# RWKV attention and capacity-limited experts: the attention output kept in fp32 columns, cast per expert, with grams in halves and logits in spare PSUM columns

## The chip, the cores and the metric

One core of one Trainium2 chip. The time is the device time of one execution in microseconds (us); each run gives its own time, and a profile of one execution is a little shorter than the time of that run. Below, "time" is the median over runs, and "span" is the length of the profiled execution.

## The reference, cut to what matters

```python
def _attn_ref(r, k, v, w, u):            # r, k, v, w: (4, 8, 768, 48), u: (8, 48)
    for t in range(S):
        cur = einsum('bhd,bhe->bhde', u[None] * kt, vt)
        y[:, :, t] = einsum('bhd,bhde->bhe', rt, state + cur)
        state = wt[:, :, :, None] * state + einsum('bhd,bhe->bhde', kt, vt)

def _moe_ref(x, w_gate, w1, w2):         # x: (3072, 384), E = 8, F = 1024, cap = 384
    logits = x @ w_gate
    # greedy over all (token, expert) pairs by falling logit: a token goes to the
    # first expert that still has room; each expert takes exactly 384 tokens
    ...
    for e in range(E):
        h = np.maximum(x[mask] @ w1[e], 0.0)
        out[mask] = h @ w2[e]
```

So there are three stages: an attention scan that yields x, an assignment that needs all logits, and eight experts that each gather 384 rows of x, apply two products, and scatter the rows.

## The kernel before

The engines are named as the profile names them: PE is TensorE, ACT is ScalarE, DVE is VectorE, POOL is GpSimd. Tiles whose names end in `ps` lie in PSUM, where the products of PE are written; the others lie in SBUF. The attention works in 24 units (6 chunks of 128 positions, 4 batches each). In a unit, the gram is the product of its transposed keys and receptances, the mask copy takes the allowed part of it out of PSUM, and the intra products apply that part to the values. Every engine has its own list of operations, ordered by a key: unit number times a period, plus an offset for the kind of operation. The parts that the change touches, with cuts marked:

```python
# attention, per unit u
add("G", u, "PE", ...)        # gram: 32 matmuls into Gps
add("MS", u, "DVE", ...)      # mask copy of the whole gram, Gps -> M
add("Y", u, "PE", ...)        # intra products from M, then the last state product, into Yps
add("XE", u, "ACT", ..., fn=lambda u=u: nc.scalar.copy(             # contiguous, fp32
        out=XF[slot(("xf", u))][:112].rearrange("p s j t -> p s (j t)"),
        in_=Yps[:112, :, :256]))
add("XB", u, "ACT", ..., fn=lambda u=u: nc.scalar.copy(             # cast to bf16 columns
        out=xTb[:112, u].rearrange("p (s t) j -> p s j t", s=2),
        in_=XF[slot(("xf", u))][:112]))
...                                          # logits from XF, in a transpose tile (Tps)

# zeroes in the weight tiles of the later experts, then their loads (issued on GpSimd)
for e in range(NEARLY, E):                   # NEARLY = 3
    weights[e] = weight_tiles(wp, e)
    nc.scalar.activation(out=weights[e][0][32:64], ..., func=AF.Copy, scale=0.0)
    for fn in _weight_loads(nc, e, *weights[e], moe_w1, moe_w2):
        fn()

# experts
def gather(e):
    xe = xes[e] = xp.tile([128, NPAIR, CAP], BF16, name="xe", tag="xe")
    for k in range(2):
        nc.gpsimd.indirect_copy(
            xe[:, :, k * 192:(k + 1) * 192].rearrange("p j s -> p s j"), data, ...)
def up(e): ...      # 8 groups of 4 matmuls, 4 PSUM tiles hps; relu on ScalarE and VectorE in turn
def down(e): ...    # 3 groups of 8 matmuls, copy to osb, scatter (indirect DMA issued on GpSimd)

gather(0)
gather(1)
for e in range(E):
    up(e)
    if e + 2 < E:
        gather(e + 2)
    if e:
        down(e - 1)
down(E - 1)
```

## Time and profile before

The median was 437.4 us.

| stage (profile of before, span 441.3 us) | from | to |
|---|---|---|
| attention, up to the start of the last copy of logits | 0 | 159.4 |
| assignment, up to the ready index tile | 159.7 | 203.6 |
| experts, from the ready index on | 203.6 | 441.3 |

The page's summary rows. In section 2 each digit is the busy share of one of 40 equal slices (11 us each) in tenths; PEclk is the granted clock of TensorE in tenths.

```profile
span 441.3 us, 9730 instructions
...
PE   3878289898997663442060829370823708239000
...
POOL 8987835555559624420344433424335243352220
PEclk9999769999999655555566778685685956759655
```

Two things are to be seen: a weak slice near 50 us in which PE drops to 2 and the clock to 7 and 6 after it, and an expert stage in which PE comes in bursts while POOL is never quite idle.

Groups by line (line, engine, operation, output<-input, shapes, count, then busy us and mean ns of one, then the engine's idle time just before it and who ended it):

```profile
L725 PE MATMUL hps<-xe,w 112*128 112x384 bf16 x256 | 63.2, 426 | 111.5 <-POOL xe L715 111.5
L715 POOL INDIRECT_COPY xe<-xTb,idx 128x768 bf16 x16 | 61.8, 3864 | 106.2 <-issue 106.2
L428 ACT CAST xTb<-xf 112x512 bf16<-112x512 f32 x24 | 32.4, 1352 | 1.1
L424 ACT COPY xf<-yps 112x512 f32<-112x512 f32 x24 | 14.1, 587 | 27.8 <-PE yps L384 27.6
```

PE waits 111.5 us for gathered rows: POOL sets the pace of the expert stage. The gather is shown with 3.86 us, and nearly as much again stands as "issue" in front of it. "Perfetto Trace Analysis" of the Trainium skill (section "GPSIMD Engine Instruction") says to time such instructions by their start-to-start spacing. The trace agrees that this is needed: gathers in a row start 9.72 us apart while some 3.9 us is shown. The timeline of POOL around one expert (start, duration, then in brackets the idle time before and what ended it):

```profile
269.28 3.90 POOL L715 INDIRECT_COPY xe<-xTb,idx 128x768 bf16 x1 [5.82 <-issue]
279.00 3.91 POOL L715 INDIRECT_COPY xe<-xTb,idx 128x768 bf16 x1 [5.82 <-issue]
282.77 1.09 POOL L745 DMA_INDIRECT out_dram<-osb,tok_i  x1
286.25 1.00 POOL L745 DMA_INDIRECT out_dram<-osb,tok_i  x1 [2.39 <-issue]
289.63 0.97 POOL L745 DMA_INDIRECT out_dram<-osb,tok_i  x1 [2.38 <-PE hps L725]
296.90 3.85 POOL L715 INDIRECT_COPY xe<-xTb,idx 128x768 bf16 x1 [6.30 <-issue]
```

The first scatter follows the gather with no wait. In the attention, the waits view between 40 and 65 us names the cause of the weak slice (who waits, for whom, us in total, times, the longest):

```profile
PE tps L437 <- DMA wgT<-in_moe_w_gate_dram: 9.3, 2, 5.9
```

The pace of the attention is read from the copies out of yps. Those of unit 7 and of unit 19, twelve units apart:

```profile
67.60 0.59 ACT L424 COPY xf<-yps 112x512 f32<-112x512 f32 x1 [0.48 <-PE yps L384]
...
131.44 0.59 ACT L424 COPY xf<-yps 112x512 f32<-112x512 f32 x1
```

(131.44 - 67.60) / 12 = 5.32 us per unit (by chunks of four units it varies from 5.0 to 5.5). Last, VectorE between the two stages: the assignment (nl) starts straight after the last logits.

```profile
159.43 0.19 DVE L451 COPY logits_sb<-tps 128x32 f32<-128x32 f32 x1 [4.97 <-PE tps L448]
159.71 0.26 DVE L495 TENSOR_SCALAR nl<-logits_sb 128x192 f32<-128x192 f32 x1
```

### The profile page before, as it was taken

Reading aid. Unit: us, or ns where it says so; the run is one execution under the profiler, and the core shown is the slowest. Engines: PE = TensorE matmul, PEld = TensorE weight load, DVE = VectorE, ACT = ScalarE, POOL = GpSimd, SP = SyncE. Lnnn points to the kernel's source line nnn. Section 1 sums busy time; section 2 is a strip of 40 time slices with the busy share of each in tenths; the row PEclk is TensorE's granted clock in tenths of the full one; section 3 lists DMA queues with packets and bytes.
Section 4 is the critical chain, followed back from the end, with each engine's and each line's share of the span. In section 5 each row is a group of like instructions: output and inputs, shape, how many; then the busy total and the mean of one; then the engine's idle time right before and its main releaser. Section 6 shows DMA issues by size and latency. Waiting matters only on the chain. (4 is left out here: it accounts for less than half of the span.)

```text
span 441.3 us, 9730 instructions
## 1 busy us (share of the span) xinstructions
PE 238.5 (54%) x4221; PEld 151.9 (34%) x4221; DVE 149.0 (34%) x379; ACT 141.5 (32%) x196; POOL 206.8 (47%) x177
## 2 busy tenths in 40 slices
PE   3878289898997663442060829370823708239000
PEld 2556166566665531231030415140411404115000
DVE  4666238776785437664010202020200202003000
ACT  3687348776886379000010102010100102001000
POOL 8987835555559624420344433424335243352220
PEclk9999769999999655555566778685685956759655
DMA  9997999898408989998000000000100001001110
GB/s 167 171 175 141 178 184 172 157 186 159 77 3 129 202 121 186 192 202 120 0 0 0 0 0 2 18 36 0 56 0 18 36 0 54 1 18 72 56 53 19
DMA packets 113918, 37.06 MB, mean 84 GB/s; under 512 B 101328, under 2 KB 109648, under 8 KB 113872
## 3 DMA queue, kind: packets, MB, share of 16 engines
q1 hardware_dynamic: 100432, 19.09, 24.3%
q0 software_dynamic: 13440, 17.31, 21.6%
q8 instruction: 35, 0.57, 0.5%
q14 instruction: 11, 0.09, 0.1%
HBM read 44.25 MB, written 4.72 MB: 111 GB/s over the span
## 5 line engine op out<-in xcount | busy, mean ns | idle before, releaser
L725 PE MATMUL hps<-xe,w 112*128 112x384 bf16 x256 | 63.2, 426 | 111.5 <-POOL xe L715 111.5
L715 POOL INDIRECT_COPY xe<-xTb,idx 128x768 bf16 x16 | 61.8, 3864 | 106.2 <-issue 106.2
L725 PEld LDWEIGHTS <-w 112*128 112x128 bf16 x256 | 31.5, 123 | 144.0 <-issue 136.1
L728 DVE TENSOR_SCALAR hsb<-hps 128x384 bf16<-128x384 f32 x32 | 17.9, 558 | 159.6 <-PE hps L725 159.6
L730 ACT ACTIVATE hsb<-hps 128x384 bf16<-128x384 f32 x32 | 15.7, 491 | 165.6 <-PE hps L725 165.6
L314 POOL TENSOR_TENSOR mm<-diag,dd 128x512 f32<-128x512 f32 x24 | 25.7, 1071 | 42.1 <-DVE dd L309 20.4
L745 POOL DMA_INDIRECT out_dram<-osb,tok_i x24 | 23.6, 985 | 46.0 <-DMA out_dram<-osb,tok_i 21.4
L326 PE MATMUL tps<-ident,krs 128*112 128x128 f32 x192 | 33.3, 298 | 4.2 <-DVE krs L295 3.0
L331 ACT COPY krT<-tps 112x512 f32<-112x512 f32 x48 | 30.2, 629 | 8.6 <-PE tps L326 8.4
L428 ACT CAST xTb<-xf 112x512 bf16<-112x512 f32 x24 | 32.4, 1352 | 1.1
L738 PE MATMUL ops<-w,hsb 128*128 128x384 bf16 x192 | 32.4, 326 | 0.0
L690 POOL DMA_DIRECT2D w<-in_moe_w_dram x32 | 18.6, 583 | 25.9 <-DMA w<-in_moe_w_dram 13.7
L301 POOL TENSOR_TENSOR rku<-kr 128x384 f32<-128x384 f32 x24 | 24.1, 1004 | 1.4 <-DMA kr<-in_r_dram 1.2
L403 DVE COPY_PREDICATED mm<-mask,gps 128x512 f32<-128x512 uint8 x24 | 17.4, 726 | 21.0 <-PE gps L398 14.7
L305 POOL TENSOR_TENSOR rku<-rku,u_bc 128x384 f32<-128x384 f32 x24 | 24.1, 1004 | 0.3
L326 PEld LDWEIGHTS tps<-ident,krs 128*112 128x112 f32 x192 | 20.9, 140 | 8.8 <-POOL rku L301 3.7
L384 PE MATMUL yps<-krT,sm 48*48 48x64 f32 x384 | 22.5, 233 | 2.2 <-issue 1.5
L282 PE MATMUL cps<-ww,negut 128*128 128x384 f32 x48 | 21.4, 529 | 4.3 <-ACT ww L242 4.3
L295 DVE TENSOR_TENSOR krs<-kr,cps 128x768 f32<-128x768 f32 x24 | 22.7, 946 | 2.3 <-ACT cps L290 2.0
L384 PE MATMUL yps<-krT,st 48*48 48x64 f32 x384 | 22.4, 233 | 1.9 <-issue 1.9
L738 PEld LDWEIGHTS <-hsb 128*128 128x128 bf16 x192 | 18.8, 98 | 12.4
L424 ACT COPY xf<-yps 112x512 f32<-112x512 f32 x24 | 14.1, 587 | 27.8 <-PE yps L384 27.6
(144 smaller groups left out, 389.7 us busy)
## 6 DMA issues: line engine op xcount, KB each, us to landing
w<-in_moe_w_dram POOLq DMA_DIRECT2D x32, 192.0 KB, 10.1
w<-in_moe_w_dram POOLq DMA_DIRECT2D x8, 768.0 KB, 13.0
ww<-in_w_dram SPq DMA_DIRECT2D x24, 192.0 KB, 4.9
kr<-in_k_dram SPq DMA_DIRECT2D x24, 192.0 KB, 4.6
kr<-in_r_dram SPq DMA_DIRECT2D x24, 192.0 KB, 4.7
vv<-in_v_dram SPq DMA_DIRECT2D x24, 192.0 KB, 5.0
out_dram<-osb,tok_i POOLq DMA_INDIRECT x24, 2.6
u_bc<-in_u_dram SPq DMA_DIRECT2D x1, 192.0 KB, 4.3
```

Source lines behind the costliest of these rows:

```text
L295: fn=lambda u=u, kr=kr, b=b: nc.vector.tensor_tensor(out=KR[slot(("kr", u))][:, :, :, :D], in0=kr[:, :, b, :].rearrange("t x (h d) -> t x ...
L301: fn=lambda u=u, kr=kr, b=b: nc.gpsimd.tensor_tensor(out=P[slot(("p", u))], in0=kr[:, 0, b, :], in1=kr[:, 1, b, :], op=ALU.mult))
L305: fn=lambda u=u: nc.gpsimd.tensor_tensor(out=P[slot(("p", u))], in0=P[slot(("p", u))], in1=u_bc, op=ALU.mult))
L314: fn=lambda u=u: nc.gpsimd.tensor_tensor(out=M[slot(("m", u))], in0=_free(diag, [0, 2], [0, NPAIR], [1, 64]), in1=_free(Dg[slot(("dg", u)) ...
L326: nc.tensor.transpose(t[:112, at:at + 128], pair_of(s[:, x], j), ident)
L331: nc.scalar.copy(out=KRT[slot(("krt", u))][:112, 2 * half:2 * half + 2].rearrange("p j x t -> p (j x t)"), in_=Tps[slot(("t", u, half))][: ...
L384: mm(Yps[q * 64:q * 64 + D, half, j * 64:(j + 1) * 64], lhsT=s, rhs=t[cc * 64:cc * 64 + D, j, 1, half * 64:half * 64 + 64], start=(i == 0 ...
L428: fn=lambda u=u: nc.scalar.copy(out=xTb[:112, u].rearrange("p (s t) j -> p s j t", s=2), in_=XF[slot(("xf", u))][:112]))
L715: nc.gpsimd.indirect_copy(xe[:, :, k * 192:(k + 1) * 192].rearrange("p j s -> p s j"), data, idx16[:, e * 24 + k * 12:e * 24 + (k + 1) * 1 ...
L725: nc.tensor.matmul(hps, lhsT=w1sb[:112, jj, f8 * 128:(f8 + 1) * 128], rhs=xe[:112, jj, :], start=(jj == 0), stop=(jj == 3))
L738: nc.tensor.matmul(ops_, lhsT=hsb[:, f8, pc * 128:(pc + 1) * 128], rhs=w2sb[:, f8, :], start=(f8 == 0), stop=(f8 == FC - 1))
L745: nc.gpsimd.indirect_dma_start(out=out, out_offset=bass.IndirectOffsetOnAxis(ap=tok_i32[:, j:j + 1], axis=0), in_=osb, in_offset=None)
```

## The change

Its intent: drop the second pass over the attention output (the bf16 cast), let the gather move whole fp32 columns of four neighbouring values, and cast only what an expert needs; let PE start the intra products after half a gram; free the transpose tiles of logits. The keys of the schedule were tuned again with it. The diff, cut to its core:

```diff
-        add("MS", u, "DVE", 730, after=[op["G", u], op["DG", u]], ...)     # one gram, mask copy, intra
+        for i in range(2):                                                 # two halves of each
+            add(f"G{i}", u, "PE", 290, gram, ...)
+            add(f"MS{i}", u, "DVE", 430, after=[op[f"G{i}", u], op["DG", u]], ...)
...
-        add("XE", u, "ACT", 590, ... XF ..., in_=Yps[:112, :, :256]))
-        add("XB", u, "ACT", 620, ... xTb ...)
+        add("XE", u, "ACT", 620, after=[op["Y1", u]], give=[("y", u)],
+            fn=lambda u=u: nc.scalar.copy(
+                out=xT[:, u].rearrange("p (s t) j -> p s j t", s=2),       # fp32, 16-byte stride
+                in_=Yps[:, :, :256].rearrange("p s (j t) -> p s j t", j=NPAIR)))
...
-                t = Tps[slot(("l", c))]                       # logits in a transpose tile
+                t = Ctail[0]                                  # spare columns of the cumsum tile
...
-            add("SW", u, "DVE", 500, ...)                     # state times decay
+            add("SW", u, "POOL", 600, ...)
...
     def gather(e):
         xe = xes[e] = xp.tile([128, NPAIR, CAP], BF16, name="xe", tag="xe")
         for k in range(2):
-            nc.gpsimd.indirect_copy(xe[...].rearrange("p j s -> p s j"), data, ...)
+            at = slice(k * 192, (k + 1) * 192)
+            x4 = gp.tile([128, 192, NPAIR], FP32, name="x4", tag="x4")
+            nc.gpsimd.indirect_copy(x4, data, ...)
+            flip = x4.rearrange("p s j -> p j s")
+            nc.vector.tensor_copy(out=xe[:, :2, at], in_=flip[:, :2])
+            nc.scalar.copy(out=xe[:, 2:, at], in_=flip[:, 2:])
...
     gather(0)
-    gather(1)
     for e in range(E):
+        if e + 1 < E:
+            gather(e + 1)
         up(e)
-        if e + 2 < E:
-            gather(e + 2)
         if e:
             down(e - 1)
...
-NEARLY = 3
+WT_AT = [30.0 + 0.01 * i for i in range(10)]                  # weights of the first two experts
+NEARLY = 2
...
-            nc.scalar.activation(out=weights[e][0][32:64], ..., func=AF.Copy, scale=0.0)
+            nc.vector.memset(weights[e][0][32:64], 0.0)
```

## The prediction

> **What bounds the kernel now.** Three stages, read from the timeline.
>
> Attention, 0 to 160 us. The q/k/v/w loads run at a DMA share of 0.9 to 1.1 until 113 us; from 62 us on PE is 18 of 20 us busy and one unit (the copy out of yps) takes 5.3 us. A hole at 45 to 62 us: the first logits matmul waits 9.3 us for the gate weights, queued behind loads (waits view).
>
> Assignment, 160 to 204 us: a DVE chain of short instructions.
>
> Experts, 205 to 433 us: POOL alone. PE waits 111.5 us for xe. Gathers end 9.72 us apart (shown as 3.85 busy after 5.86 "issue"), three scatters cost 8.2 us; 16 gathers (155 us) and 24 scatters follow each other without a gap. ACT and DVE are mostly idle there.
>
> **What the change does, by stage.**
>
> Attention. It removes the cast to xTb (24 x 1.35 us ACT), the xTb memsets (10.7 us POOL), 128-column transposes for four-column results, and the gate-weight hole. Halved grams let PE start the intra products earlier. SW moves to POOL, which has room. The logits leave the tps buffers. Against it: the yps copy now writes fp32 at a stride of 16 bytes, and the logits matmul reads at that stride. The cast, which writes bf16 at a stride of 8 bytes, takes 1.35 us where the same-sized plain copy takes 0.59; I estimate 0.6 to 1.1 us for the strided fp32 copy. Loads alone need 113 us, PE about 4.7 us per unit. Estimate: logits complete at 140 us (133 to 150) instead of 160.
>
> Between stages. Six zero memsets of expert weights move from ACT to DVE, ahead of the assignment in DVE's order. The built order shows 2048 elements each. "VectorE: DVE Perf Modes" of the Trainium skill (section on zero memsets) says one cycle per element: an estimate of 2.2 us each, 13 us on the critical path. Before they cost nothing (ACT, 17.6 us, idle engine). So about 7 us of the attention gain remain.
>
> Experts. Two opposite terms.
> (a) The gather writes contiguous fp32 instead of bf16 at a stride of 768 bytes. I read 5.86 us as fetching and 3.85 us as writing, 5 ns for each of 768 elements, slow like the strided bf16 cast on ACT. Contiguous writes should cut it: estimate 6.9 us per gather, saving 45 us over 16.
> (b) The casts of expert e+1 stand before the relus of expert e on DVE and ACT. Only four hps buffers exist, so up(e) stops after four groups until gather e+1 has landed; then cast 0.6, relu 0.5, four groups of 1.0, the first down group 1.4 and its copy 0.6 pass before the first scatter of e-1. Estimate: POOL now waits 7 us per expert, six times, 43 us. Before, the scatters followed at once.
> So the expert stage comes out about even; it is 40 us longer if the gather does not get faster.
>
> **Prediction:** 431 us, range 411 to 476. Faster by over 2%: 0.45; within 2%: 0.27; slower: 0.28.
>
> **What would show it.** Right: gather spacing near 7 us; POOL idle about 7 us before the first scatter of each expert; DVE 13 us in memsets before the assignment; no hole at the first logits; units nearer 5 us; last logits near 140 us. Wrong: gather spacing still 9.7 us (about 475 us); the yps copy at 1.4 us or more, with PE waiting for it; logits matmuls far above 1.9 us per chunk; POOL not waiting at the scatters.
>
> **What would make it wrong.** The gather's write phase may be a software loop indifferent to stride and type. The strided fp32 copy may cost more than the cast it replaces and hold yps, so that attention gains nothing. The granted clock, 0.5 to 0.76 outside steady attention, scales (b).

## The result, and the profile after

The kernel after takes 470.64 us (468.41 to 473.04, 4 runs) against 437.67 us. The ratio is 1.0745, 95% interval 1.0659 to 1.0832: slower. Ratios here and below are the mean time of one kernel's runs over that of the other's of the same rounds, so not quite the ratio of the medians quoted. Executions over 1.5% slower than the fastest of the same kernel are left out of the means.

```profile
span 471.3 us, 9781 instructions
...
PE   4786888888888603344046450620902705308900
...
POOL 4689283835657264310101020111120210210320
PEclk9997999969999855555565795675765956856965
```

POOL's digits in the expert stage fell from mostly 2 to 4 down to 0 to 3, and yet the stage is longer. The groups that answer to those of before:

```profile
L733 PE MATMUL hps<-xe,w 112*128 112x384 bf16 x256 | 62.1, 415 | 136.5 <-ACT hsb L738 119.0
L724 DVE CAST xe<-x 128x384 bf16<-128x384 f32 x16 | 39.8, 2486 | 109.5 <-POOL x L720 109.5
L720 POOL INDIRECT_COPY x<-xT,idx 128x768 f32 x16 | 17.2, 1077 | 119.8 <-issue 113.4
L432 ACT COPY xT<-yps 128x512 f32<-128x512 f32 x24 | 26.3, 1098 | 37.4 <-PE yps L386 37.4
```

The gather itself shrank to 1.08 us shown. PE no longer waits for the gather but for a relu of its own expert on ScalarE (119.0 us). The timeline of POOL around one expert says why:

```profile
319.13 1.08 POOL L720 INDIRECT_COPY x<-xT,idx 128x768 f32 x1 [6.30 <-issue]
327.34 1.07 POOL L720 INDIRECT_COPY x<-xT,idx 128x768 f32 x1 [7.13 <-issue]
337.86 1.01 POOL L753 DMA_INDIRECT out_dram<-osb,tok_i  x1 [9.45 <-DVE osb L752]
341.29 0.97 POOL L753 DMA_INDIRECT out_dram<-osb,tok_i  x1 [2.42 <-issue]
344.64 0.97 POOL L753 DMA_INDIRECT out_dram<-osb,tok_i  x1 [2.38 <-DMA out_dram<-osb,tok_i]
351.91 1.07 POOL L720 INDIRECT_COPY x<-xT,idx 128x768 f32 x1 [6.31 <-issue]
```

POOL stands still for 9.45 us before the first scatter. The casts of expert e+1 stand ahead of the relus of expert e in the order of ScalarE and VectorE, so up(e) stops once its four PSUM tiles are full, until gather e+1 has landed. Only then do relu, the second half of up(e), down(e-1) and the scatter follow, and meanwhile POOL has nothing to do. Six such waits: 8.68, 7.82, 9.45, 8.31, 8.02 and 9.27 us, 51.6 us in all. VectorE between the stages:

```profile
162.26 0.19 DVE L453 COPY logits_sb<-cps 128x32 f32<-128x32 f32 x1 [0.67 <-PE cps L450]
162.93 1.76 DVE L926 MEMSET w<- 32x2048 uint32 x1 [0.48 <-DVE logits_sb L453]
...
173.64 1.76 DVE L926 MEMSET w<- 32x2048 uint32 x1 [0.38 <-issue]
175.43 0.26 DVE L496 TENSOR_SCALAR nl<-logits_sb 128x192 f32<-128x192 f32 x1
```

Where the 30.0 us between the two spans lie, each from the starts and ends in the two traces and rounded by itself:

| piece | before | after | change, us |
|---|---|---|---|
| up to the start of the last logits copy | 159.4 | 162.3 | +2.8 |
| from there to the start of the assignment | 0.3 | 13.2 | +12.9 |
| assignment | 43.9 | 43.5 | -0.4 |
| index ready to the end of the first gather | 11.2 | 8.4 | -2.8 |
| end of the first gather to the end of the last | 177.9 | 196.7 | +18.7 |
| end of the last gather to the end | 48.5 | 47.2 | -1.3 |

In the attention, the hole at the first logits is gone, but PE waits for the mask copies twice in a unit. The waits view of PE in 60 to 150 us:

```profile
PE gps L347 <- DVE mm L409: 9.0, 16, 0.6
PE yps L423 <- DVE mm L409: 4.8, 14, 0.4
```

In the same view of before these two waits were 2.8 us (8 times, L345) and 2.1 us (twice, L416): 4.9 us, now 13.8 us. There is also a new hole near 37 us: a zero memset of weights (3.50 us) stands in POOL's order ahead of an operand that the mask copy needs. First POOL's line, then PE's:

```profile
34.51 3.50 POOL L906 MEMSET w<- 32x4096 bf16 x1
...
40.63 1.11 PE L423 MATMUL yps<-mm,vv 64*48 64x64 f32 x32 [3.81 <-DVE mm L409]
```

In this profile the clock was at half speed for two stretches of the attention, about 39 to 46 us and 97 to 107 us.

### The profile page after: what moved, and what is told of

Same layout as the page of the kernel before. It is cut to its first block, busy times and chain, and to the rows that moved or that the text cites. A ratio compares the mean times of both kernels' runs of the same rounds, so it can differ in the third digit from the quotient of the medians.

```text
span 471.3 us, 9781 instructions
## 1 busy us (share of the span) xinstructions
PE 240.8 (51%) x4247; PEld 156.2 (33%) x4247; DVE 190.8 (40%) x407; ACT 117.7 (25%) x183; POOL 158.0 (34%) x190
## 5 line engine op out<-in xcount | busy, mean ns | idle before, releaser
L733 PE MATMUL hps<-xe,w 112*128 112x384 bf16 x256 | 62.1, 415 | 136.5 <-ACT hsb L738 119.0
L724 DVE CAST xe<-x 128x384 bf16<-128x384 f32 x16 | 39.8, 2486 | 109.5 <-POOL x L720 109.5
L720 POOL INDIRECT_COPY x<-xT,idx 128x768 f32 x16 | 17.2, 1077 | 119.8 <-issue 113.4
L725 ACT CAST xe<-x 128x384 bf16<-128x384 f32 x16 | 13.9, 867 | 149.7 <-POOL x L720 149.7
L432 ACT COPY xT<-yps 128x512 f32<-128x512 f32 x24 | 26.3, 1098 | 37.4 <-PE yps L386 37.4
L409 DVE COPY_PREDICATED mm<-mask,gps 128x256 f32<-128x256 uint8 x48 | 20.8, 443 | 33.2 <-PE gps L402 17.6
L333 ACT COPY krT<-tps 112x512 f32<-112x512 f32 x48 | 28.7, 600 | 17.6 <-PE tps L328 16.6
L328 PEld LDWEIGHTS tps<-ident,krs 128*112 128x112 f32 x192 | 23.8, 147 | 12.7 <-issue 7.4
L423 PE MATMUL yps<-mm,vv 64*48 64x64 f32 x768 | 21.1, 229 | 12.9 <-DVE mm L409 11.6
L284 PE MATMUL cps<-ww,negut 128*128 128x384 f32 x48 | 22.9, 563 | 7.7 <-ACT ww L245 6.8
L746 PEld LDWEIGHTS <-hsb 128*128 128x128 bf16 x192 | 19.3, 101 | 13.8 <-issue 2.1
L292 ACT ACTIVATE cps<-cps 128x768 f32<-128x768 f32 x24 | 19.2, 802 | 16.6 <-PE gps L402 9.1
## 6 DMA issues: line engine op xcount, KB each, us to landing
w<-in_moe_w_dram POOLq DMA_DIRECT2D x8, 768.0 KB, 13.8
```

The source lines that it names most:

```text
L284: mm(Cps[:, 0, :DX], lhsT=negut, rhs=ww[:, b, :], start=True, stop=True)
L328: nc.tensor.transpose(t[:112, at:at + 128], pair_of(s[:, x], j), ident)
L333: nc.scalar.copy(out=KRT[slot(("krt", u))][:112, 2 * half:2 * half + 2].rearrange("p j x t -> p (j x t)"), in_=Tps[slot(("t", u, half))][: ...
L432: fn=lambda u=u: nc.scalar.copy(out=xT[:, u].rearrange("p (s t) j -> p s j t", s=2), in_=Yps[:, :, :256].rearrange("p s (j t) -> p s j t", ...
L724: nc.vector.tensor_copy(out=xe[:, :2, at], in_=flip[:, :2])
L733: nc.tensor.matmul(hps, lhsT=w1sb[:112, jj, f8 * 128:(f8 + 1) * 128], rhs=xe[:112, jj, :], start=(jj == 0), stop=(jj == 3))
```

## The experiments

Theory 1: the loss in the expert stage is the order of the casts. Theory 2: 13 us of it are the memsets on VectorE. Theory 3, on the attention: some part of the rework costs as much as the rest gains. The rivals are named in each expectation. The first four ran beside before at 438.67 us (437.96 to 439.36, 7 runs).

### e_late_casts: the casts of expert e+1 after the work of e

```diff
-            flip = x4.rearrange("p s j -> p j s")             # in gather(): cast at once
+            x4s[e].append(x4)
+    def cast(e): ...                                          # the same two casts per half
     gather(0)
+    cast(0)
     for e in range(E):
         ...
         up(e)
         if e:
             down(e - 1)
+        if e + 1 < E:
+            cast(e + 1)
```

> The changed kernel with one edit: the two casts of expert e+1 stand after the relus and copies of up(e) and down(e-1) in DVE's and ACT's order, no longer before them. Theory 1 (the casts' place in the order holds up POOL): the 7.8 to 9.5 us that POOL waits before the first scatter of experts 0 to 5 (51.6 us in all) vanishes, so about 420 us, 50 us less than the changed kernel. Rival (PE's up and down work itself is what the scatters wait for, whatever the order): the wait stays above 4 us per expert and the time stays above 445 us.

Measured: correct, 426.79 us (423.71 to 429.04, 4 runs), ratio 0.9706 (0.9666 to 0.9745). The scatter follows the gather at once:

```profile
264.69 1.08 POOL L719 INDIRECT_COPY x<-xT,idx 128x768 f32 x1 [6.51 <-issue]
265.96 1.32 POOL L758 DMA_INDIRECT out_dram<-osb,tok_i  x1 [0.18 <-issue]
```

Theory 1 holds. The order of the casts costs 44 us by the medians (470.64 - 426.79), and with that one edit the change is faster than before. What follows also is that the rest of the change, taken together, was worth having.

### e_memset_act: the six memsets back on ScalarE

```diff
-            nc.vector.memset(weights[e][0][32:64], 0.0)
+            nc.scalar.activation(out=weights[e][0][32:64], ..., func=AF.Copy, scale=0.0)
```

> The changed kernel with the six zero memsets moved from DVE back to ACT (the old activation with scale 0). Theory 1: they lie on the critical path between the last logits copy and the negation of the logits; these two then follow each other at once, and 13 us come off, about 458 us. Rival: the stretch between is set by something else, for instance the weights' arrival, and less than 4 us come off.

Measured: correct, 460.07 us median (453.47 to 466.96, 5 runs, two of them slow), ratio 1.0337 (1.0316 to 1.0358). The profiled run is one of the slow ones, so only intervals that do not hang on PE are read from it. The assignment starts 0.2 us after the last logits copy (165.82 to 166.04), so the 13 us are gone. But GpSimd was still issuing weight loads until 213.9 us when the index was ready at 209.4 us, and from the ready index to the end of the first gather it took 11.9 us instead of 8.4. So 3.5 us were given back. Theory 2 holds, with a new neighbour on the chain.

### a_whole: grams, mask copies and intra products whole again

```diff
-        for i in range(2):
-            add(f"G{i}", ...); add(f"MS{i}", ...); add(f"Y{i}", ...)
+        add("G", u, "PE", 580, ...); add("MS", u, "DVE", 730, ...); add("Y", u, "PE", 710, ...)
```

> The changed kernel with grams, masked copies and intra products whole again. Theory 1 (the halves cost more than they bring: PE waits for DVE twice per unit, 0.56 us at the state product and 0.34 us at the second half): the last logits copy comes 6 to 14 us earlier than at 162.4 us, total about 461 us. Rival (the halves are harmless or help, and attention is held by other things): the last logits copy stays within 3 us or comes later.

Measured: correct, 466.35 us (464.63 to 468.98, 4 runs), ratio 1.0638 (1.0591 to 1.0686), last logits copy at 157.3 us. The wait for the mask copies did not change with their size. In the view of PE in 60 to 150 us it is 13.5 us now, once a unit, against 9.0 and 4.8 us in two parts:

```profile
PE yps L418 <- DVE mm L405: 13.5, 16, 0.9
```

### a_xw_late: GpSimd's zero memsets after the last unit

```diff
-    "Zy": -60000, "Xw": -20000, "Wt": 0,
+    "Zy": -60000, "Xw": 76000, "Wt": 0,
```

> The changed kernel with the two 3.5 us zero memsets of expert weights on POOL moved from units 4 and 5 to after the last unit's POOL work. Theory 1 (the first holds up the u product, so the mask copy, so PE idles 3.8 us at 37 us, and the granted clock falls to 0.5 for the next 4 us): the hole at 37 us vanishes with the clock dip after it, and the last logits copy comes 4 to 9 us earlier, total about 464 us. Rival: the loads set the pace there (DMA share 1.0) and the gain is below 2 us.

Measured: correct, 467.73 us (465.71 to 469.69, 4 runs), ratio 1.0665 (1.0621 to 1.0709), last logits copy at 158.2 us. The hole at 37 us is gone. A half-clock stretch came at 117 to 128 us instead of the one at 97 to 107.

The ratios of both runs overlap with the interval of after, so at this point neither was a clean answer. The next four ran beside before at 440.09 us (438.5 to 444.13, 7 runs).

### b_gate_early: the kernel before, its gate weights loaded first

```diff
-    ..., "Lu": -34000, "Lg": 0, ...
+    ..., "Lu": -34000, "Lg": -33000, ...
```

> The kernel before, with one thing changed: the gate's weights are loaded at the head of the load queue instead of behind other loads. In the profile of before, the first logits product waits 9.3 us for that load and the attention has a hole from 45 to 62 us, followed by a half-speed clock. If that hole is a loss that the new schedule of the change could win back, the last logits copy comes 8 to 12 us earlier (about 148 to 151 instead of 159.4 us) and the time falls to about 427 us. Rival: the hole is covered by the loads, which end only at 113 us; then the last logits copy moves by less than 4 us.

Measured: correct, 436.19 us (434.74 to 437.58, 4 runs), ratio 0.99 (0.9849 to 0.9952): the same at 2%. The last logits copy came at 153.7 us, 5.7 us earlier, between the two expectations. So the hole that the change removes was worth 4 to 6 us (4 by the medians, 5.7 in the profiles) and not the 12 that the wait and its clock suggested.

### a_xe_flat: contiguous copy and contiguous logits operand (wrong result)

```diff
-                out=xT[:, u].rearrange("p (s t) j -> p s j t", s=2),
-                in_=Yps[:, :, :256].rearrange("p s (j t) -> p s j t", j=NPAIR)))
+                out=xT[:, u].rearrange("p t j -> p (t j)").rearrange("p (s x) -> p s x", s=2),
+                in_=Yps[:, :, :256]))
...                                                           # and the logits' rhs read to match
```

> The kernel after, with the attention output copied from PSUM contiguously instead of with a stride of 16 bytes, and the logits product reading it contiguously. The result is wrong on purpose (the gather then reads a wrong order). Theory that the strided copy and strided moving operand slow the attention: copies fall from 1.10 to about 0.59 us, logits products from 349-406 to about 250-350 ns a matmul, and the last logits copy comes 5 to 12 us earlier than 162.3 us. Rival, that both are hidden behind the PE's waits for the mask copies: the copies are faster, but the last logits copy moves by less than 2 us and so does the time (470.6 us).

Measured: wrong as intended (relative error 1.17), 464.52 us (461.59 to 466.42, 4 runs), ratio 1.0538 (1.0476 to 1.06), last logits copy at 153.7 us. The copies fell from 1.10 to 0.59 us and the logits matmuls from 406 to 276 ns. The strided layout is therefore not hidden. How much of it is pace and how much is clock is taken up below.

### e_late_act: late casts, both halves on ScalarE

```diff
 # on top of e_late_casts
-            nc.vector.tensor_copy(out=xe[:, :2, at], in_=flip[:, :2])
+            nc.scalar.copy(out=xe[:, :2, at], in_=flip[:, :2])
```

> The kernel after with late casts, as in the run before with late casts (426.8 us), but with both halves of each cast on ScalarE. If the 6.84 us casts on VectorE come from sharing a port with the running gather, there is no cast of over 1.5 us left, the start-to-start spacing of every pair of gathers is 7.52 us (it is 8.20 us for later pairs), and the time is about 3 to 5 us under late casts alone, some 422 to 424 us. Rival, that the 8.20 us have another cause (for instance weights landing in SBUF): spacing stays at 8.20 us and the time within 1.5 us of 426.8, or above it as ScalarE now carries both halves.

The casts on VectorE had shown a spread that a cast should not have. In the line view of the kernel after (min, median and max in ns):

```profile
L724 DVE CAST xe<-x x16: 496/516/6843, 227.4 to 424.1; 128x384 bf16<-128x384 f32 x16
```

The long ones start at the end of the first gather of a pair and end when the fetch part of the second one ends, and those second gathers come 8.20 us after the first instead of 7.52. "SBUF — State Buffer" of the Trainium skill (section "Who interferes with whom") says that VectorE, in some of its instructions, and GpSimd share one port pair as a lock that one of them holds for a whole instruction, and that ScalarE never waits for it. Measured: correct, 412.91 us (411.95 to 418.86, 4 runs, one of them slow), ratio 0.9365 (0.931 to 0.942). The line view of the casts, and two gathers of a later pair:

```profile
L729 ACT CAST xe<-x x16: 858/863/887, 220.4 to 371.3; 128x384 bf16<-128x384 f32 x16
```

```profile
317.73 1.07 POOL L719 INDIRECT_COPY x<-xT,idx 128x768 f32 x1 [6.30 <-issue]
325.04 1.07 POOL L719 INDIRECT_COPY x<-xT,idx 128x768 f32 x1 [6.23 <-issue]
```

No cast is long any more, and every back-to-back pair of gathers is 7.29 to 7.31 us apart: less than the 7.52 us that we took for undisturbed. So even a short cast on VectorE had held a gather up by 0.23 us. The trace agrees with the page. The gain was larger than expected. From the first gather's start to the end it is 190.9 us against 200.4 us with the casts on both engines, 9.5 us; the spacing gives 5 x 0.23 + 5 x 0.91 = 5.7 us of it. Most of the rest lies in the scatters up to the last gather: waits before them that are 2.1 us shorter in all, and first scatters of some 1.01 instead of 1.25 us. Another 7.6 us in the profiles are an earlier end of the attention, in whose code nothing differs. That leads to the clock.

### The clock, from the runs so far

TensorE's granted clock is 1.00 or 0.50 in these traces. "TensorE: Matmul & The Clock Gate" of the Trainium skill (Part 1) has the same two states and says that idle windows of about 3.4 us bring on the slow one. The traces agree with the states (1.00 and 0.50) and, after the holes, with the cause: in the kernel after, the clock is 0.50 from 39.15 us on, within PE's idle 3.81 us. Before the later stretches they show no such hole. In the kernel after the clock falls at 97.18 us, and in the 7 us before that PE has no gap of over 0.56 us. It was less busy, 2.33 of the last 3.41 us, but from 121.07 to 124.48 us it was busy for 2.14 of 3.41 us and the clock stayed at 1.00, so that share does not settle it.

Let the clock loss of a run be the sum of 4 us x (1 - granted clock) over the 4-us windows from 36 to 144 us. Four profiled runs have the same attention code:

| run | clock loss, us | last logits copy starts |
|---|---|---|
| after | 8.6 | 162.3 |
| e_late_casts | 8.5 | 162.8 |
| e_memset_act | 10.2 | 165.8 |
| e_late_act | 1.3 | 155.2 |

The end of the attention follows the clock loss nearly one for one. With one profile a run, a difference in the end of an attention of less than some 8 us can be the clock alone. A measure free of it is the pace over whole chunks at full clock. In e_late_act it is read as for before, from units 7 and 19:

```profile
59.98 1.11 ACT L432 COPY xT<-yps 128x512 f32<-128x512 f32 x1 [0.50 <-PE yps L386]
...
130.33 1.11 ACT L432 COPY xT<-yps 128x512 f32<-128x512 f32 x1 [0.51 <-PE yps L386]
```

| attention | units read, all at full clock | us per unit | against after's code, 12 units |
|---|---|---|---|
| before | 7 to 19 | 5.32 | -6.5 us |
| b_gate_early | 7 to 19 (from 62.81 to 126.61 us) | 5.32 | -6.5 us |
| after's code (in e_late_act) | 7 to 19 | 5.86 | |
| a_whole | 11 to 19 (from 88.14 to 133.57 us) | 5.68 | -2.2 us |
| a_xe_flat | 7 to 19 (from 63.90 to 132.05 us) | 5.68 | -2.2 us |
| a_logits_tps (next) | 7 to 19 (from 63.97 to 137.65 us) | 6.14 | +3.4 us |

Units 11 to 19 of after's code take 5.89 us each in e_late_act and, again at full clock, in e_memset_act, so the pace repeats from run to run. It may not be multiplied by all 24 units: the last four, 19 to 23, take 20.2 us in the kernel after and in e_late_act (clock 1.00), but 24.6 us in before, at a mean clock of 0.79.

### a_logits_tps: logits and decay transposes back in the transpose tiles

```diff
-                t = Ctail[0]
+                t = Tps[slot(("l", c))]
...                                                           # likewise LE, LT, LF, WT, WE; keys moved
```

> The kernel after with one part undone: logits, their transposes and the decay transposes use the two transpose tiles of PSUM again, as in the kernel before, instead of spare columns of the cumulative-sum tile. If sharing the cumulative-sum tile costs (the decay copy on VectorE waits for the logits products 10.5 us in four waits in the profile of after), those waits vanish and the last logits copy comes 3 to 8 us earlier than 162.3 us. Rival: the spare columns do pay, since the transposes are then not held up by logits; then the last logits copy is at the same time or later, and the time is 470 us or more.

Measured: correct, 470.8 us (470.14 to 472.38, 4 runs), ratio 1.0692 (1.0639 to 1.0744), last logits copy at 161.2 us with a clock loss of only 3.4 us. The waits of the decay copy for logits vanish, and the pace is 6.14 us per unit. The rival holds for the edit as a whole: the spare columns with their keys (four keys moved in this run) pay about 0.28 us per unit, although they bring a visible wait. In c_wt_tps below, which puts back the decay transposes alone, units 7 to 19 take 6.00 us each at full clock, so about half of it belongs to those.

The next three ran beside before at 439.7 us (434.94 to 441.21, 7 runs).

### c_all: the best parts together

```diff
 # on top of e_late_act
-            nc.vector.memset(weights[e][0][32:64], 0.0)
+            nc.scalar.activation(out=weights[e][0][32:64], ..., func=AF.Copy, scale=0.0)
-    "Zy": -60000, "Xw": -20000, "Wt": 0,
+    "Zy": -60000, "Xw": 46600, "Wt": 0,
-WT_AT = [30.0 + 0.01 * i for i in range(10)]
+WT_AT = [11.62 + 0.005 * i if i < 4 else 12.0 + 0.3 * (i - 4) for i in range(10)]
...                                                           # loads of expert 7 after gather(2)
```

> The best parts together: late casts on ScalarE, the zeroing of the six later weight tiles back on ScalarE, the zeroing of the first two on GpSimd moved to its idle time at about 120 us, the first two experts' weights loaded from there on (their DMA queues are idle from 106 us), the last expert's weights asked for after the third expert's gathers. Worked out from the profile of late casts on ScalarE (410.2 us): 13 us less because the routing starts at the last logits copy, of which 0 to 3 us may be given back if the loads' issue on GpSimd is still late; the rest as it was. Span about 398 us with an attention end at 156 us, time 393 to 406 us. If the time is above 408 us, the memsets' 13 us are again given back and that term is not additive.

Measured: correct, 413.4 us (409.31 to 417.52, 4 runs, the profiled one slow), ratio 0.9398 (0.9319 to 0.9478). A miss. Yet from the last logits copy to the start of the first gather as shown it took 51.1 us, against 64.1 us in e_late_act: the memsets' 13 us were all there. The expert stage had grown from 190.9 to 198.4 us.

### c_all_whole: the same with whole products

```diff
 # on top of c_all, the edit of a_whole
-            add(f"G{i}", ...); add(f"MS{i}", ...); add(f"Y{i}", ...)
+        add("G", u, "PE", 580, ...); add("MS", u, "DVE", 730, ...); add("Y", u, "PE", 710, ...)
```

> The same with grams, mask copies and intra products whole again, as in the kernel before. If the halves cost by themselves, the last logits copy is 2 to 5 us earlier than in the run of the best parts at an equal clock loss, and so is the time (about 395 us). Rival, that the 4.7 us that whole products gained in the first try were a matter of where the clock fell: within 1.5 us of each other once the clock loss is taken off.

Measured: correct, 408.21 us (405.88 to 409.27, 4 runs), ratio 0.9293 (0.9229 to 0.9357). It is 1.1% under c_all, as a_whole (1.0638) is 1.0% under after (1.0745), with this around the first scatters:

```profile
249.60 1.08 POOL L752 DMA_INDIRECT out_dram<-osb,tok_i  x1 [0.30 <-issue]
259.23 1.00 POOL L752 DMA_INDIRECT out_dram<-osb,tok_i  x1 [8.54 <-issue]
```

Its last logits copy is at 157.4 us with a clock loss of 1.7 us, that of c_all at 166.1 with 6.8: 3.6 us earlier once the clock loss is taken off, as expected. The time of about 395 us was missed. Whole products are better by some 4 to 5 us by both pairs of times, and the pace goes the same way (5.71 us in units 7 to 19 here), though the intervals of each pair overlap, so this size is likely and not proved. The 8.54 us are what c_all lost: the second scatter waits, and the load held back for expert 7 had just been issued from the same engine.

### c_wt_tps: the decay transposes back in a transpose tile

```diff
 # on top of c_all: WT as four transposes a chunk instead of 40 matmuls of 4 columns in all
-                    mm(Ctail[1][:112, ...], lhsT=pair_of(Ws[c % 2], j), rhs=sel4, ...)
+                    nc.tensor.transpose(t[:112, j * 128:(j + 1) * 128], pair_of(Ws[c % 2], j), ident)
```

> The best parts, with only the decay transposes (40 matmuls of 4 columns in the change) made four transposes a chunk in a transpose tile again. Of seven profiled kernels with the narrow matmuls, five had a second stretch of half clock between 70 and 128 us that begins at or near them, and of three with the transposes none. If the narrow matmuls bring it on, this run has no second stretch, its clock loss between 36 and 144 us is under 4 us, and its times spread less. Rival: the stretch comes by chance, and it can be here as well; or the transposes, having to share two tiles with the key transposes, cost more than they save.

Measured: correct, 415.42 us (411.11 to 417.17, 4 runs), ratio 0.9489 (0.9423 to 0.9555). The only half-clock stretch of the attention came at 135 to 142 us and began in a hole of 2.49 us in PE (from 133 us); between 70 and 128 us there was none, and the clock loss was 3.4 us, as the theory asked. The times spread nearly as before. Over all runs, six of ten profiled kernels with the narrow matmuls had a stretch between 70 and 128 us, and none of four with the transposes. That fits the theory and does not prove it, since c_all_whole and c_final have the narrow matmuls and no such stretch. What triggers the later stretches stays open.

### c_final: c_all_whole without holding a load back

```diff
 # c_all_whole asked for expert 7's weights after gather(2); now in the loop with the others
-            held = _weight_loads(nc, e, *weights[e], moe_w1, moe_w2)
-            if e + 1 < E:
-                for fn in held:
-                    fn()
+            for fn in _weight_loads(nc, e, *weights[e], moe_w1, moe_w2):
+                fn()
```

> The best parts with whole products, as before, but the last expert's weights are asked for ahead of the gathers again. In the two runs of the best parts that held them back, the second scatter of the first expert waited 8.54 us instead of 3.93 us, and the three weight loads and this wait together made the expert stage 7.4 us longer (198.4 against 190.9 us from the first gather to the end). Theory: the scatters queue behind the held weight load, so without it the expert stage takes 190.9 us again, and with whole products the span is about 399 to 403 us, the time 398 to 405 us. Rival: the earlier start of the expert stage makes it meet the weight loads either way; then the gain is given back, the first gather comes later by as much, and the time stays at 408 us.

Measured: correct, 398.83 us (396.48 to 401.48, 6 runs), beside before at 438.42 us (435.67 to 440.42, 11 runs); ratio 0.9109 (0.9073 to 0.9145).

```profile
242.38 1.08 POOL L752 DMA_INDIRECT out_dram<-osb,tok_i  x1 [0.19 <-issue]
245.85 0.99 POOL L752 DMA_INDIRECT out_dram<-osb,tok_i  x1 [2.39 <-ACT hsb L737]
```

The second scatter waits 2.39 us instead of 8.54, and the expert stage takes 394.7 - 204.6 = 190.1 us, as expected. So the held load did cost 7 to 9 us. That the scatter stood behind it in a DMA queue, and not behind some other thing that the load did, fits but was not separated. This profile had no clock loss at all between 36 and 144 us, and its last logits copy is at 153.3 us. This version beats both kernels: 9% under before and 15% under after by the medians (398.83 against 470.64 us, from different calls).

## Why the prediction was right or wrong

The time, 470.64 us, lies inside the range (411 to 476), near its upper end. The middle, 431 us, was 40 us too low, and "faster" was given more weight than "slower", which came. That the range held is in part luck: its upper end stood for a gather that stays at 9.7 us, which did not happen, and the attention's missing gain filled that room. The terms of the sum:

| term, as the prediction put it | predicted, us | measured, us | verdict |
|---|---|---|---|
| logits complete at 140 instead of 160 | -20 | +2.8 | mis-sized, the largest error |
| six memsets before the assignment | +13 | +12.9 | right |
| gather 6.9 instead of 9.7 us, over 16 | -45 | -32 (11 at 7.52, 5 at 8.20) | right in kind, 13 us too large |
| POOL waits 7 us before six scatters | +43 | +51.6 | right in kind, 9 us too small |

These errors sum to 23 + 13 + 9 = 45 us. Some 5 us of other differences of the expert stage go the other way; no run was spent on them.

**The step that failed: "units nearer 5 us ... logits complete at 140 us (133 to 150)".** The pace at full clock went from 5.32 to 5.86 us per unit. The prediction added up what the engines no longer had to do: a cast on ScalarE and memsets on GpSimd, both of which had room. It did not ask where PE would wait for VectorE, with which it alternates on the gram and its mask copy. The runs put figures on the pieces at full clock. Halving costs 0.18 us per unit (a_whole; 0.21 over the same units 11 to 19). It was meant to let PE start earlier, but PE waits for mask copies 13.8 us in 90 us with halves, 13.5 us without, and 4.9 us in before, whose order has other work for PE there. So that wait came with something other than the halves, and they did not shorten it. The strided copy and the strided logits operand cost 0.18 (a_xe_flat). The spare columns with their keys give back 0.28 (a_logits_tps). If such pieces add, undoing the first two leaves 5.50 us, not the 5.32 us of before; the remaining 0.18 us per unit was not taken apart. The new keys, with the waits that they leave, are the first suspect, and the state product moved to GpSimd another; no run put the old keys under the new parts. The removal of the hole was a gain, but one of about 5 us (b_gate_early).

Between the two profiles, the +2.8 us add up like this. Unit 7 comes out 5.1 us earlier (62.46 against 67.60 us): the hole. Units 7 to 19 take 10.9 us longer (74.7 against 63.8 us), 6.5 us of it by the pace; the rest fits the clock, whose mean was 0.93 against 1.00. Units 19 to 23 take 4.3 us less, since before ran them at a mean clock of 0.79. The last logits copy comes 1.4 us later after the last unit. So part of the loss was hidden by before's own clock. Without most of the clock loss, in e_late_act, the same attention code has its last logits copy at 155.2 us: still 15 us after the 140 of the prediction.

**The memsets** came out as put: 1.76 us shown each and 2.14 us apart, against an estimate of 2.2 us from "VectorE: DVE Perf Modes" of the Trainium skill (section "Zero memsets can be issued as uint32 (trn2)"). They were on the critical path, as e_memset_act and c_all show.

**The gather** did get faster with its new output: shown 1.08 instead of 3.85 us. Layout and type changed together, so which of them did it was not separated. The write part was guessed to shrink by 2.8 us, and it did (3.85 - 1.08 = 2.77). What was missed lies in the fetch: in the undisturbed gathers of e_late_act 6.22 us, 0.4 us more than the 5.82 us of before, and up to 7.13 us where VectorE's cast ran into it. The prediction had no term for VectorE and GpSimd getting into each other's way.

**The stall** was read rightly from the order of the engines before anything ran. The order of the casts was said to cost 43 us, the waits were 51.6 us, and moving the casts gained 44 us. The prediction set it against the gather as a balance, as it had to for the kernel as written; but the two are independent, and the order was free to be mended.

## What to carry to other kernels

Put a conversion in an engine's order after the work that frees the bottleneck engine, not where its input is made: in-order engines turn an early wait into everybody's wait (here 51.6 us of waits on POOL). Keep casts like these off VectorE while GpSimd gathers, if ScalarE has room. And judge a schedule by its pace over whole periods at full clock, and then look whether the first and last periods keep it: the end time of one profile moved by 10 us between runs of the same attention code.

## What the Trainium skill lacked or had wrong

- "SBUF — State Buffer", section "Who interferes with whom": the lock is as stated, and casts are named among those that can take it. Which of the two engines gets it could not be told from the page: in the kernel after, casts that all start within 0.04 us of a gather's end took about 0.5 us in the first five pairs of gathers, with the next gather 0.23 us later than without them (7.52 against 7.30 us), and 6.84 us in the five later pairs.
- "GPSIMD Engine Reference" has no time for an indirect copy. Here 192 indices of 4 elements (768 per partition) cost 9.72 us with a bf16 output at a stride of 768 bytes, and 7.30 us with a contiguous fp32 output and VectorE out of the way; 6.2 us of it pass before the shown part begins.
- "TensorE: Matmul & The Clock Gate", Part 1, puts the slow clock down to idle windows. Runs of one attention code had 1.3 to 10.2 us of clock loss, and some half-clock stretches began without such a window (in after at 97.18 us, with no gap of PE over 0.56 us in the 7 us before). What starts those is neither on the page nor settled here.
- "SBUF — State Buffer" says that accesses which cross into a new 16-byte line pay a penalty. ScalarE's copy of 512 fp32 elements took 0.59 us contiguous and 1.10 us at a stride of 16 bytes, which agrees; but a cast of the same size to bf16 at a stride of 8 bytes took 1.35 us, more although two elements share a line. The cast also reads SBUF and converts, where the copy reads PSUM, so the stride is not the only difference.
